# The high and low parts of the stationary operands of a gated FFN, laid element by element beside each other

## The chip, the core and the metric

The kernel runs on one core of a Trainium2 chip. The core has a matrix engine (PE, whose weight loads are shown apart as PEld), a vector engine (DVE), a scalar engine (ACT), a general engine (POOL) and a queue that issues transfers (SP). The metric is the device time of one launch in microseconds (us), the median of several runs. A matmul of PE takes two operands from on-chip memory: the stationary one (up to 128 × 128), which a weight load (LDWEIGHTS) puts into the array beforehand, and the moving one (up to 512 columns wide), which then streams past it. The result lands in PSUM.

## What is computed

First a chunked scan over sequences of 768 positions (4 batches, 8 heads, head size 32, state size 16), whose result is reshaped to 3072 tokens × 256. Then a gated FFN on these tokens, with 1536 hidden units:

```python
def reference(**kwargs):
    attn_out = _attn_ref(**attn_kwargs)              # (4, 8, 768, 32)
    x = attn_out.transpose(0, 2, 1, 3).reshape(B * S, H * D)   # (3072, 256)
    gate = 1.0 / (1.0 + np.exp(-(x @ w_gate)))       # w_gate (256, 1536)
    val = x @ w_val
    return (gate * val @ w_out).astype(np.float32)   # w_out (1536, 256)
```

The weights of the FFN arrive as 64-bit floats; the kernel turns them into 32-bit parts itself.

## The kernel before

The sequence is cut into 6 chunks of 128 positions, and a chunk of all 4 batches gives 512 tokens. The scan of a chunk (24 "units", one per chunk and batch) is made of small matmuls with work of DVE, ACT and POOL between them (lines 429 to 599), ahead of the chunk's FFN. PE does the FFN chunk by chunk, and the units of the next chunk are threaded in between. Chunk number is k, block of 128 hidden units is f (12 of them), and batch is j.

Precision decides the form of a matmul. From f = 6 of chunk 0 on, gate and value use pairs of parts: a value is held as a high part in the 32-bit format fp32r and a low part, what is left over, in the same format. Three products replace one: high × high, high × low, low × high. Some work of chunk 0 uses whole fp32 numbers instead.

- Gate and value, f < 6 of chunk 0 (lines 788 and 882): the stationary operand is a slice of the whole weights (tile `wr`), moving is `xw`, both fp32.
- Gate and value after that (line 891 in `products_of`): the stationary operand is a 128 × 128 slice of the parts `w` of a weight tile; moving are the parts `xh` and `xl` of the chunk's tokens, 512 columns. Six matmuls give one tile of 512 in PSUM, for the gate (`pg`) and then for the value (`pv`).
- From these, ACT makes the sigmoid `g` (832), DVE multiplies it with the value (853), ACT writes the high part of `h` (857) and POOL the low part (859). In chunk 0 DVE writes `h` whole, as fp32 (816, 849).
- Projection, chunk 0 (line 918 in `proj`): the stationary operand is a slice of the whole `h`, moving are whole weights, 256 columns.
- Projection of chunks 1 to 5: the stationary operand is the high part of `h`, moving are both parts of the weights side by side, 512 columns (929); then the low part of `h` under the high part of the weights, 256 columns (930). For the last 128 tokens the low part comes at the end (926, 937).

The parts of the weights are made by `part_w`: ACT writes the high part (390), POOL the low part (392), for 18 weight tiles, 12 of gate and value and 6 of the projection. A weight tile holds 2 × 256 numbers per partition and part. The whole weights from which they come lie in every second 32-bit word of their tile, since they are made in place from 64-bit numbers; so the matmuls of lines 788 and 882 read a stationary operand with a step of 8 bytes, and those of line 918 a moving one.

A planner (`run`) sets the order of all instructions when the program is built, from costs and due times; nothing of it is decided on the chip. Each engine then works through its list in order. Tiles of `h` and `w` lie in one pool (`hp`) under fixed tags, in buffers of 4 KiB per partition, which are reused from chunk to chunk.

The tiles that the change touches are made in these lines:

```python
w = hp.tile([P, 2, NK, 2 * P], F32R, ...)     # parts_of: part, k, column
hs[0, f] = hp.tile([P, 512], F32, ...)        # half_value and value: h of chunk 0, whole
hs[k, f] = hp.tile([P, 2, 512], F32R, ...)    # value: part, token
```

Of the kernel before, what the change touches and what calls it, by code (L numbers as in the profile page):

```python
# [8 lines left out]
F32 = mybir.dt.float32  # L9
F32R = mybir.dt.float32r  # L10
# [61 lines left out]
def tile_ssd_then_gated_ffn(  # L72
# [11 lines left out]
    nc = tc.nc  # L84
    NB, H, S, D = x.shape
    N = Bm.shape[-1]
    DM, DF = w_gate.shape
    wg32, wv32, wo32 = (w.bitcast(U32) for w in (w_gate, w_val, w_out))
    P = 128
# [5 lines left out]
    NK = DM // P  # L95
    NF = DF // P
# [9 lines left out]
    place = {i: n for n, i in enumerate(order)}  # L106
# [4 lines left out]
    hp = ctx.enter_context(tc.tile_pool(name="hp", bufs=1))  # L111
# [75 lines left out]
    def step(eng, cost, needs=(), makes=(), port=False, **buffers):  # L187

        return eng, cost, needs, makes, port, buffers
# [141 lines left out]
    raws, wgv, wo = {}, {}, {}  # L331
# [61 lines left out]

    def parts_of(i):
        if i < NF:
            w = hp.tile([P, 2, NK, 2 * P], F32R, tag=f"s{place[i]}", name=f"w{i}")
            wgv[i] = w
            return w[:, 0], w[:, 1]
        w = hp.tile([P, 2, 2, DM], F32R, tag=f"s{place[i]}", name=f"w{i}")
        wo[i - NF] = w  # L400
        return w[:, :, 0, :], w[:, :, 1, :]
# [359 lines left out]
    hs, xb, xw = {}, {}, []  # L761
# [12 lines left out]
    def thin(k, f):  # L774
        return k == 0 and f < NPLAIN

    def single(k, f):
        return k == 0 and f < NWHOLE

    def halved(k, f):  # L780
        return k == 0 and f < NHALF
# [24 lines left out]
    def half_value(f, i):  # L806
        yield step(
            "pe", GV0 / 2, [("whole", f // 2 * 2 + 1), ("pg", 0, f, i)], [("pv", 0, f, i)] + half_used(f, i, 1), port=8, banks=1
        )
        pm = half_of(f, i, 1)  # L810
        yield step("dve", DVE_HALF, [("sig", 0, f, i)], [("h", 0, f, i)], banks=-1, g=-1)
        g = gs.pop((0, f, i))
        if (0, f) not in hs:
            hs[0, f] = hp.tile([P, 512], F32, tag=f"h{f}", name=f"h0_{f}")
        by = "p (b l) -> p b l"
        nc.vector.tensor_tensor(
            out=hs[0, f].rearrange("p (b s l) -> p b s l", b=NB, s=2)[:, :, i], in0=pm[:, : 2 * P].rearrange(by, b=NB),
            in1=g[:, : 2 * P].rearrange(by, b=NB), op=ALU.mult,
        )

    def half_used(f, i, j):
        return [("used", f // 2 * 2 + j, i)] if f % 2 else []

    def all_used(q):
        return [("used", q, i) for i in range(2)] if q < NHALF else [("used", q)]
# [8 lines left out]
    def value(k, f):  # L834
        makes = [("pv", k, f)] + ([("gv", k)] if f == NF - 1 else [])
        yield step("pe", GV0 if thin(k, f) else GV_T / 2, needs_of(k, f, 1) + [("pg", k, f)], makes + used(k, f, 1), port=8 if thin(k, f) else 12, banks=1)
        pm = products_of(k, f, 1)
        held = []
        if k == 0:
            held = {  # L840
                4: [("S", b) for b in range(NB)], 5: [("cb", 1)], 6: [("cb", 3), ("cd", 2), ("cd", 3)],
                7: [("scan", 3)], 8: [("p",)], 9: [("a_p",)], 10: [("a_z",)],
            }.get(f, [])
            held += [n for i in range(NPLAIN) for n in all_used(i)] + [("xp", 1)] if f == NF - 1 else []
        if single(k, f):
            yield step("dve", DVE_MM, [("sig", k, f)] + held, [("h", k, f)], banks=-1, g=-1)
            g = gs.pop((k, f))
            hs[k, f] = hp.tile([P, 512], F32, tag=f"h{f}", name=f"h{k}_{f}")
            nc.vector.tensor_tensor(out=hs[k, f], in0=pm, in1=g, op=ALU.mult)
            return  # L850
        yield step("dve", DVE_MM, [("sig", k, f)], banks=-1)
        g = gs.pop((k, f))
        nc.vector.tensor_tensor(out=g, in0=pm, in1=g, op=ALU.mult)  # L853
        eng = yield step(("act", "dve"), (ACT_SB, DVE_1), [("proj", k - 1)] + held)
        hs[k, f] = hp.tile([P, 2, 512], F32R, tag=f"h{f}", name=f"h{k}_{f}")
        hh, hl = (hs[k, f][:, i] for i in range(2))
        copies[eng](hh, g)  # L857
        eng = yield step(("dve", "pool"), (DVE_SB, POOL_SB), [], [("h", k, f)], port=True, g=-1)
        engines[eng].tensor_tensor(out=hl, in0=g, in1=hh.bitcast(F32), op=ALU.subtract)  # L859

    def used(k, f, j):
        return [("used", f // 2 * 2 + j)] if thin(k, f) and f % 2 else []
# [12 lines left out]
    def products_of(k, f, j):  # L875

        fs = slice(f % 2 * P, (f % 2 + 1) * P)
        pm = ps_mm.tile([P, 512], F32, tag="mm", name=f"p{'gv'[j]}{k}_{f}")
        if thin(k, f):

            for kt in range(NK):
                nc.tensor.matmul(  # L882
                    pm, whole[f // 2 * 2 + j][:, kt, fs], xw[0][:, kt], start=(kt == 0), stop=(kt == NK - 1)
                )
            return pm
        xh, xl = xb[k]
        w = wgv[f // 2 * 2 + j]
        i = 0
        for kt in range(NK):
            for part, xx in ((0, xh), (0, xl), (1, xh)):  # L890
                nc.tensor.matmul(pm, w[:, part, kt, fs], xx[:, kt], start=(i == 0), stop=(i == 3 * NK - 1))  # L891
                i += 1
        return pm

# [2 lines left out]
    def proj(k, j):  # L897

        js = slice(j * P, (j + 1) * P)
        last = (k, j) == (NCH - 1, NB - 1)  # L900
        fs = [f for f in range(NF) if not single(k, f)] + [f for f in range(NF) if single(k, f)]
        for n, f in enumerate(fs):
            start, stop = n == 0, n == NF - 1
            if n % 4 == 0:
                some = fs[n : n + 4]
                needs = [n for i in some for n in ([("h", k, i, 0), ("h", k, i, 1)] if halved(k, i) else [("h", k, i)])]
                needs += sorted({("whole" if single(k, i) else "w", NF + i // 2) for i in some})
                if n == 0:
                    needs.append(("gv", k))
                yield step(  # L910
                    "pe", 0.92 if last else sum(0.45 if single(k, i) else PROJ_T / 12 for i in some), needs,
                    [("proj", k)] if j == NB - 1 and n + 4 == NF else [],
                    port=8 if last else 16, banks=int(n == 0),
                )
                if n == 0:
                    acc = ps_mm.tile([P, 512], F32, tag="mm", name=f"po{k}_{j}")
            if single(k, f):
                nc.tensor.matmul(  # L918
                    acc[:, :DM], hs[k, f][:, js], whole[NF + f // 2][:, f % 2], start=start, stop=stop,
                    skip_group_check=True,  # L920
                )
                continue
            hh, hl = (hs[k, f][:, i, js] for i in range(2))
            w = wo[f // 2][:, f % 2]
            if last:
                nc.tensor.matmul(acc, hh, w.rearrange("p i m -> p (i m)"), start=start, stop=stop)  # L926
                continue

            nc.tensor.matmul(acc, hh, w.rearrange("p i m -> p (i m)"), start=start, stop=False, skip_group_check=True)  # L929
            nc.tensor.matmul(acc[:, :DM], hl, w[:, 0, :], start=False, stop=stop, skip_group_check=True)  # L930
        o = wk.tile([P, DM], F32, tag="o", name=f"o{k}_{j}")
        if last:

            yield step("pe", 1.4, [], [("end",)], port=24, banks=1)
            low = ps_mm.tile([P, 512], F32, tag="mm", name="po")
            for f in range(NF):
                nc.tensor.matmul(
                    low[:, :DM], hs[k, f][:, 1, js], wo[f // 2][:, f % 2, 0, :], start=(f == 0), stop=(f == NF - 1)
                )
        if single(k, NF - 1):  # L940
            eng = yield step(("act", "dve"), (ACT_HALF, DVE_HALF), [], [], o=1, banks=-1)
            copies[eng](o, acc[:, :DM])
        else:
            yield step("act", ACT_HALF, [], [], o=1)
            nc.scalar.copy(o, acc[:, :DM])  # L945
            yield step("dve", DVE_HALF, banks=-1)
            nc.vector.tensor_tensor(out=o, in0=acc[:, DM:], in1=o, op=ALU.add)  # L947
        if last:
            yield step("dve", DVE_HALF)
            nc.vector.tensor_tensor(out=o, in0=low[:, :DM], in1=o, op=ALU.add)  # L950
        row = j * S + k * L
        yield step("sp", 0.52, port=0.4, o=-1)
        nc.sync.dma_start(out[row : row + P, :], o)
# [205 lines left out]
```

## Time and profile before

| | us |
|---|---|
| median of 3 runs | 370.71 |
| lowest, highest | 369.96, 372.96 |
| span of the profiled execution | 368.7 |

The profiled execution is one execution of the program under the hardware profiler, and no time of its own beside the span is known. The span reaches from its first to its last instruction, and is what the shares and the sums below refer to; the runs also hold what lies around it, so that the median is 2.0 us above the span.

The chunks lie in it as follows: gate and value of chunk 0 until 63 us, its projection until 89.8, then gate and value and projection of the chunks 1 to 5 by turns, the last projection from 348.4 on.

How to read the views: durations are those of single instructions; matmuls are pipelined, so that a matmul starts before the one ahead of it has drained, and durations of matmuls add up to more than the time that they take. The distance between two starts is the pace. "x" is a count. Behind the bar of a group stands the time for which the engine was idle just before such an instruction, and who ended it. A weight load has rows of its own under PEld and overlaps matmuls.

### The profile page before, as it was taken

To read this page: it belongs to the slowest core of one execution; us is meant where nothing else is said; L and a number is where in the kernel's file an instruction comes from. 1 tells how busy PE (TensorE), PEld (TensorE's weight loads), DVE (VectorE), ACT (ScalarE), POOL (GpSimd) and SP (SyncE) were. 2 spreads that over 40 slices of the span, in tenths; PEclk is the share of its full clock that TensorE was granted. 3 is DMA by queue.
4 is the path that set the end of the run, shared out by engine and by line. 5 is a ranking of instruction groups with operands and counts; after the bars stand their busy time and mean duration, and the time that the engine had idled before them with its cause. 6 is when DMAs were issued, how large, how long until landed. Compare 5 with 4: busy or idle time off the path is not lost.

```text
span 368.7 us, 8115 instructions
## 1 busy us (share of the span) xinstructions
PE 360.1 (98%) x3372; PEld 285.9 (78%) x3372; DVE 156.4 (42%) x278; ACT 150.2 (41%) x309; POOL 151.9 (41%) x160
## 2 busy tenths in 40 slices
PE   8989899999999999999999999999999999999996
PEld 3568378778887788778788887888877888888885
DVE  4778478675325751253452225422243510222201
ACT  2565985324565411544410454511445420343400
POOL 5436665746797410345420345530144240154410
PEclk9999999999999999999999999999999999999999
DMA  8999885627015331235031006321000000000000
GB/s 138 168 309 215 271 261 151 106 43 154 7 16 100 45 89 57 37 64 59 16 87 44 28 3 115 34 41 37 31 2 2 2 0 28 30 0 0 2 28 28
DMA packets 89270, 26.27 MB, mean 71 GB/s; under 512 B 76306, under 2 KB 82002, under 8 KB 89234
## 3 DMA queue, kind: packets, MB, share of 16 engines
q1 hardware_dynamic: 85074, 25.37, 30.9%
q10 hardware_dynamic: 4160, 0.39, 1.2%
q8 instruction: 26, 0.43, 0.5%
q14 instruction: 10, 0.08, 0.1%
HBM read 22.41 MB, written 3.34 MB: 70 GB/s over the span
## 4 chain that ended last, share of the span: by engine, by line
PE 87%; DMA 2%; SPq 2%; ACT 1%; DVE 1%; POOL 0%; issue 0%; POOLq 0%
PE pv L891 25%; PE pg L891 25%; PE po L929 15%; PE po L930 7%; PE po L918 6%; DMA wr<-in_moe_w_val_dram 2%; PE pcb L524 2%; PE pcb L579 2%; PE pcb L493 2%; SPq L299 1%; PE pcb L535 1%; PE pt L429 1%; PE po L926 1%; PE pv L882 1%; PE pt L430 1%; ACT wr L373 0%
## 5 line engine op out<-in xcount | busy, mean ns | idle before, releaser
L859 POOL TENSOR_TENSOR h<-g,h 128x512 fp32r<-128x512 f32 x60 | 78.8, 1314 | 153.4 <-ACT h L857 152.9
L891 PE MATMUL pv<-xh,w 128*128 128x512 f32 x264 | 94.0, 397 | 0.0
L891 PE MATMUL pg<-xh,w 128*128 128x512 f32 x264 | 93.7, 395 | 0.0
L853 DVE TENSOR_TENSOR g<-pv,g 128x512 f32<-128x512 f32 x60 | 41.5, 692 | 97.1 <-PE pv L891 94.1
L929 PE MATMUL po<-w,h 128*128 128x512 f32 x228 | 81.8, 402 | 0.0
L857 ACT CAST h<-g 128x512 fp32r<-128x512 f32 x60 | 37.2, 621 | 79.6 <-DVE g L853 79.6
L930 PE MATMUL po<-w,h 128*128 128x256 f32 x228 | 63.9, 280 | 0.0
L891 PEld LDWEIGHTS pg<-xh,w 128*128 128x128 f32 x264 | 49.5, 188 | 11.1 <-issue 0.4
L891 PEld LDWEIGHTS pv<-xh,w 128*128 128x128 f32 x264 | 49.6, 188 | 10.6 <-issue 0.5
L891 PE MATMUL pv<-xl,w 128*128 128x512 f32 x132 | 51.4, 390 | 0.0
L891 PE MATMUL pg<-xl,w 128*128 128x512 f32 x132 | 51.4, 390 | 0.0
L929 PEld LDWEIGHTS po<-w,h 128*128 128x128 f32 x228 | 42.8, 188 | 10.9 <-issue 0.3
L832 ACT ACTIVATE g<-pg 128x512 f32<-128x512 f32 x68 | 40.6, 598 | 13.9 <-PE pg L891 13.4
L930 PEld LDWEIGHTS po<-w,h 128*128 128x128 f32 x228 | 43.0, 189 | 0.2
L947 DVE TENSOR_TENSOR o<-po,o 128x256 f32<-128x256 f32 x20 | 8.5, 425 | 53.6 <-ACT o L945 53.6
L945 ACT COPY o<-po 128x256 f32<-128x256 f32 x20 | 7.4, 372 | 54.5 <-PE po L930 54.0
L392 POOL TENSOR_TENSOR w<-wr,w 128x512 fp32r<-128x512 f32 x18 | 25.6, 1427 | 8.5 <-ACT w L390 8.5
L891 PEld LDWEIGHTS pg<-xl,w 128*128 128x128 f32 x132 | 24.8, 188 | 5.1 <-issue 0.2
L891 PEld LDWEIGHTS pv<-xl,w 128*128 128x128 f32 x132 | 24.8, 188 | 4.5
L375 POOL TENSOR_TENSOR wr<-wr 128x512 int32<-128x512 int32 x18 | 20.2, 1129 | 14.3 <-ACT wr L373 8.6
L448 DVE TENSOR_TENSOR_SCAN ab<-ab,delta 128x512 f32<-128x512 f32 x20 | 24.1, 1216 | 1.9 <-DMA ab<-a_z 1.4
L918 PE MATMUL po<-wr,h 128*128 128x256 f32 x96 | 23.4, 393 | 0.0
(104 smaller groups left out, 367.9 us busy)
## 6 DMA issues: line engine op xcount, KB each, us to landing
ab<-a_z SPq DMA_DIRECT2D x40, 128.0 KB
wr<-in_moe_w_gate_dram SPq DMA_DIRECT2D x6, 512.0 KB
wr<-in_moe_w_val_dram SPq DMA_DIRECT2D x6, 512.0 KB
wr<-in_moe_w_out_dram SPq DMA_DIRECT2D x6, 512.0 KB
out_dram<-o SPq DMA_DIRECT2D x24, 128.0 KB
xn<-in_x_dram SPq DMA_DIRECT2D x10, 256.0 KB
bn<-in_B_dram SPq DMA_DIRECT2D x10, 128.0 KB
cn<-in_C_dram SPq DMA_DIRECT2D x10, 128.0 KB
```

Of the source, the lines that this page charges most:

```text
L375: nc.gpsimd.tensor_tensor(out=lw.bitcast(I32), in0=hw.bitcast(I32), in1=lw.bitcast(I32), op=ALU.add)
L392: engines[eng].tensor_tensor(out=lo, in0=lw, in1=hi.bitcast(F32), op=ALU.subtract)
L448: nc.vector.tensor_tensor_scan(out=t.rearrange("p h l -> p (h l)"), data0=t.rearrange("p h l -> p (h l)"), data1=delta.rearrange("p h l -> ...
L832: nc.scalar.activation(gs[k, f], pm, AF.Sigmoid)
L853: nc.vector.tensor_tensor(out=g, in0=pm, in1=g, op=ALU.mult)
L857: copies[eng](hh, g)
L859: engines[eng].tensor_tensor(out=hl, in0=g, in1=hh.bitcast(F32), op=ALU.subtract)
L891: nc.tensor.matmul(pm, w[:, part, kt, fs], xx[:, kt], start=(i == 0), stop=(i == 3 * NK - 1))
L918: nc.tensor.matmul(acc[:, :DM], hs[k, f][:, js], whole[NF + f // 2][:, f % 2], start=start, stop=stop, skip_group_check=True,)
L929: nc.tensor.matmul(acc, hh, w.rearrange("p i m -> p (i m)"), start=start, stop=False, skip_group_check=True)
L930: nc.tensor.matmul(acc[:, :DM], hl, w[:, 0, :], start=False, stop=stop, skip_group_check=True)
L947: nc.vector.tensor_tensor(out=o, in0=acc[:, DM:], in1=o, op=ALU.add)
```

## The change

The layout of the tiles of `w` (gate and value) and `h` changes. Where the high parts of a row stood together and the low parts behind them, a high part and its low part now lie in neighbouring 32-bit words. A slice of either part then has a step of 8 bytes. The tile of `h` in chunk 0, which has no parts, gets the same step: it takes every second word of a tile twice as large. The size of the buffers doesn't grow, since the tags had room for both parts. The parts of the projection's weights, which are moving operands, stay as they are, and so do the tokens `xh` and `xl`.

```diff
     def parts_of(i):
         if i < NF:
-            w = hp.tile([P, 2, NK, 2 * P], F32R, tag=f"s{place[i]}", name=f"w{i}")
+            w = hp.tile([P, NK, 2 * P, 2], F32R, tag=f"s{place[i]}", name=f"w{i}")
             wgv[i] = w
-            return w[:, 0], w[:, 1]
+            return w[:, :, :, 0], w[:, :, :, 1]
...
         if (0, f) not in hs:
-            hs[0, f] = hp.tile([P, 512], F32, tag=f"h{f}", name=f"h0_{f}")
+            hs[0, f] = hp.tile([P, 512, 2], F32, tag=f"h{f}", name=f"h0_{f}")[:, :, 0]
...
         if single(k, f):
...
-            hs[k, f] = hp.tile([P, 512], F32, tag=f"h{f}", name=f"h{k}_{f}")
+            hs[k, f] = hp.tile([P, 512, 2], F32, tag=f"h{f}", name=f"h{k}_{f}")[:, :, 0]
...
-        hs[k, f] = hp.tile([P, 2, 512], F32R, tag=f"h{f}", name=f"h{k}_{f}")
-        hh, hl = (hs[k, f][:, i] for i in range(2))
+        hs[k, f] = hp.tile([P, 512, 2], F32R, tag=f"h{f}", name=f"h{k}_{f}")
+        hh, hl = (hs[k, f][:, :, i] for i in range(2))
...
-                nc.tensor.matmul(pm, w[:, part, kt, fs], xx[:, kt], start=(i == 0), stop=(i == 3 * NK - 1))
+                nc.tensor.matmul(pm, w[:, kt, fs, part], xx[:, kt], start=(i == 0), stop=(i == 3 * NK - 1))
...
-            hh, hl = (hs[k, f][:, i, js] for i in range(2))
+            hh, hl = (hs[k, f][:, js, i] for i in range(2))
...
-                    low[:, :DM], hs[k, f][:, 1, js], wo[f // 2][:, f % 2, 0, :], start=(f == 0), stop=(f == NF - 1)
+                    low[:, :DM], hs[k, f][:, js, 1], wo[f // 2][:, f % 2, 0, :], start=(f == 0), stop=(f == NF - 1)
```

The planner's costs and due times stay, and the order of the instructions on every engine is the same as before. The line numbers are the same in both kernels.

## The prediction

> **What bounds the kernel now.** I read the page first (busy times, clock, chain), then busy time by stage, then durations by line, and last single instructions in the timeline.
>
> ```profile
> span 368.7 us, 8115 instructions
> PE 360.1 (98%) x3372; PEld 285.9 (78%) x3372; DVE 156.4 (42%) x278; ACT 150.2 (41%) x309; POOL 151.9 (41%) x160
> PEclk9999999999999999999999999999999999999999
> PE pv L891 25%; PE pg L891 25%; PE po L929 15%; PE po L930 7%; PE po L918 6%; DMA wr<-in_moe_w_val_dram 2%; PE pcb L524 2%; PE pcb L579 2%; PE pcb L493 2%; SPq L299 1%; PE pcb L535 1%; PE pt L429 1%; PE po L926 1%; PE pv L882 1%; PE pt L430 1%; ACT wr L373 0%
> ```
>
> The matrix engine is busy 98% of the span at the full clock, and the chain that ended last runs through the matmuls of the gated FFN: L891 (gate and value), L929, L930 and L926 (projection of chunks 1 to 5), L918 (projection of chunk 0). By stage (columns: stretch, length, then busy us and count of PE, PEld, DVE, ACT, POOL; then clock, DMA share, GB/s):
>
> ```profile
> 100.00:110.00 10.00, 10.00 (x46) 8.25 (x45) 2.46 (x4) 7.02 (x14) 9.35 (x8) 1.00 0.09 9
> 127.00:204.00 77.00, 77.00 (x813) 63.50 (x798) 29.58 (x57) 23.50 (x51) 21.03 (x23) 1.00 0.29 58
> 204.00:355.00 151.00, 151.00 (x1283) 123.88 (x1282) 44.55 (x81) 56.16 (x112) 52.18 (x48) 1.00 0.10 21
> ```
>
> Where these stretches lie, PE has no idle time. So the time changes by what the change does to the pace of PE, unless another engine falls far enough behind to stop it.
>
> The change touches only the operand that PE holds still. Of those, the first stage (L788, L882) reads 8-byte-stepped weights already, so its rows price the new form. Columns here: engine, operation, count, then shortest/median/longest in ns.
>
> ```profile
> L788 PEld LDWEIGHTS pv<-xw,wr x32: 194/196/197, 17.7 to 35.7; 128*128 128x128 f32 x32
> L788 PE MATMUL pg<-xw,wr x32: 379/379/492, 15.9 to 33.9; 128*128 128x256 f32 x32
> L882 PE MATMUL pv<-xw,wr x8: 592/592/705, 37.8 to 45.1; 128*128 128x512 f32 x8
> L209 PE MATMUL fill<-eye x4: 592/594/697, 15.0 to 17.7; 128*128 128x512 f32 x4
> L918 PEld LDWEIGHTS po<-wr,h x96: 186/188/192, 62.7 to 89.6; 128*128 128x128 f32 x96
> L918 PE MATMUL po<-wr,h x96: 385/387/493, 63.0 to 89.8; 128*128 128x256 f32 x96
> L891 PEld LDWEIGHTS pv<-xl,w x132: 187/188/192, 47.1 to 347.7; 128*128 128x128 f32 x132
> L891 PE MATMUL pv<-xl,w x132: 387/389/398, 47.3 to 347.9; 128*128 128x512 f32 x132
> L929 PE MATMUL po<-w,h x228: 389/398/504, 127.1 to 362.6; 128*128 128x512 f32 x114
> L930 PE MATMUL po<-w,h x228: 274/281/284, 127.4 to 362.8; 128*128 128x256 f32 x114
> L926 PE MATMUL po<-w,h x12: 389/395/398, 358.2 to 363.6; 128*128 128x512 f32 x12
> ```
>
> L788 and L918 are both fp32, 256 columns wide. L788 (stepped stationary, moving data in contiguous runs) takes 379 ns, L918 (contiguous stationary, moving weights stepped) 387. A quick reader concludes that a stepped stationary operand saves 8 ns a matmul. Two things say otherwise. L209 holds a contiguous stationary operand under contiguous moving data, and takes 594 against 592 of L882, whose weights are stepped: the same. And the excess is there when no weights are being loaded at all. Three matmuls, each the last before a unit's small matmuls, whose loads wait:
>
> ```profile
> 18.74 0.38 PE L788 MATMUL pv<-xw,wr 128*128 128x256 f32 x1
> 19.05 0.13 PEld L493 LDWEIGHTS pcb<-bct 32*64 32x64 f32 x2 [0.33 <-ACT bct L657]
> ...
> 52.36 0.39 PE L891 MATMUL pg<-xh,w 128*128 128x512 f32 x1
> 52.68 0.13 PEld L493 LDWEIGHTS pcb<-bct 32*64 32x64 f32 x2 [0.35 <-issue]
> ...
> 66.36 0.39 PE L918 MATMUL po<-wr,h 128*128 128x256 f32 x1
> 66.68 0.11 PEld L524 LDWEIGHTS pcb<-m,xn 64*32 64x32 f32 x2 [0.35 <-DVE wr L369]
> ```
>
> Between each matmul's start and the next load nothing is loaded, yet L891 and L918 still take 0.39 us and hold up what follows by 0.32, against 0.38 and 0.31 of L788. What L891 and L918 share, and L788, L882 and L209 do not, is how fast the moving stream runs through memory. A column costs (592 − 379) / 256 = 0.83 ns in fp32 (L882, L788) and (398 − 281) / 256 = 0.46 in fp32r (L929, L930): fp32r reads its words twice as fast, and L918 reads fp32 words that lie twice as far apart. So I read the 8 to 10 ns as a cost of the moving operand, which the change leaves as it is.
>
> **The change part by part.** No instruction is added, removed or moved on any queue: PE, DVE, ACT, POOL and SP hold the same instructions in the same order. Only addresses inside tiles change.
>
> (1) Weight loads. 792 loads at L891, 228 each at L929 and L930, 12 each at L926 and L937, 96 at L918 get the step: 1,368. Each lasts 196 ns in place of 188 by L788 against L918, 8 more. That counts only where a load isn't covered by the matmul before it. Under 512 columns it is covered: L788's matmuls last 379 both next to a 196 ns load and, above, without one, and they follow each other at the pace that their columns set. Two places remain.
>
> (1a) Loads after a unit's small matmuls stand bare. The longest matmul of a line includes such a bare load: L918 493 − 387 = 106 ns and L929 504 − 398 = 106 for contiguous weights, L788 492 − 379 = 113 and L882 705 − 592 = 113 for stepped ones: 7 ns more each. The waits of the units' loads count the places:
>
> ```profile
> PEld pcb L493 <- issue: 3.5, 10, 0.4
> PEld pcb L579 <- issue: 3.2, 10, 0.4
> PEld pcb L524 <- issue: 2.9, 9, 0.4
> ```
>
> 29 × 7 ns = 0.2 us.
>
> (1b) L930's matmul is only 256 columns wide, and the load of the next L929 has to go beside it:
>
> ```profile
> 200.11 0.19 PEld L929 LDWEIGHTS po<-w,h 128*128 128x128 f32 x1
> 200.23 0.19 PEld L930 LDWEIGHTS po<-w,h 128*128 128x128 f32 x1
> 200.46 0.19 PEld L929 LDWEIGHTS po<-w,h 128*128 128x128 f32 x1
> 200.57 0.19 PEld L930 LDWEIGHTS po<-w,h 128*128 128x128 f32 x1
> ```
>
> The load beside L930 has 0.12 and 0.11 us until the next one starts. A bare load needs 106 now and 113 then. If the load sets that pace already, all 228 (and 12 of L937) lose 7 ns: 240 × 7 = 1.7 us. If the matmul sets it, 113 still fits: 0. The two gaps of 120 and 110 ns stand around 113, so only the shorter ones should lose a few ns: I take a quarter of the bound, 0.4 us.
>
> By the Trainium skill (SBUF — State Buffer, Door 1: The DMA port swizzle) reads keep full bandwidth as long as two of them fall into each 16-byte line; an 8-byte step of fp32 gives just two. By that rule (1) would be 0, and the sum 0 in place of 0.6. The trace differs from it by the 196 against 188.
>
> (2) Matmuls. Same columns, same moving operands. 0 from the argument above; the bounds are rivals A and B.
>
> (3) Writers. ACT's cast, POOL's subtraction and DVE's product of chunk 0 now write (POOL also reads) every second word.
>
> ```profile
> L859 POOL TENSOR_TENSOR h<-g,h 128x512 fp32r<-128x512 f32 x60 | 78.8, 1314 | 153.4 <-ACT h L857 152.9
> L392 POOL TENSOR_TENSOR w<-wr,w 128x512 fp32r<-128x512 f32 x18 | 25.6, 1427 | 8.5 <-ACT w L390 8.5
> L857 ACT CAST h<-g 128x512 fp32r<-128x512 f32 x60 | 37.2, 621 | 79.6 <-DVE g L853 79.6
> L390 ACT CAST w<-wr 128x512 fp32r<-128x512 f32 x18 | 11.9, 661 | 0.0
> ```
>
> L392 and L390 have one stepped operand already, and L859 and L857 none: +113 ns on POOL and +40 on ACT bound the price. So a tile of h comes at most 0.15 us later. What covers it: POOL waits 152.9 us in all for ACT's h. The cover is thinnest in chunk 1, from 100 to 110 us, where POOL is busy 9.35 of 10 because the weights' parts and h are made by turns. There 12 tiles of h at 113 ns add up to 1.4 us of lateness. Chunk 1's last h and the matmuls that go before its use:
>
> ```profile
> 128.08 1.29 POOL L859 TENSOR_TENSOR h<-g,h 128x512 fp32r<-128x512 f32 x1 [1.44 <-ACT h L857]
> ...
> 131.31 0.50 PE L929 MATMUL po<-w,h 128*128 128x512 f32 x1
> ```
>
> POOL stood idle 1.44 us before this last h, so the lateness has been made up by then; and the matmuls from 131.31 on still read h of f 4 to 7, so f 11, done at 129.37, has over 2 us to spare. With that cover gone 1.4 us would come on top; below, nothing can be gained from writers off the path. I take 0.
>
> Sum: 0.2 + 0.4 + 0 = +0.6 us, so a span of 369.3. The profiled span of 368.7 stands 2.0 below the median of the runs (370.71); with the same 2.0 around it the forecast is **371.3 us**.
>
> **Rivals.**
>
> A, faster: the stationary step, not the moving stream, makes the excess, and the change removes it. For it: L788 and L882 are the only full-width loads with the step, and the only full-width matmuls of the FFN without the excess. Against it: L209, and the excess without a load. Price: 792 × (389 − 379) = 7.9; L929 228 × (398 − 379) = 4.3; L930 at half the columns and so half of L929's excess or a little less, 228 × 9 = 2.1; L918 96 × 8 = 0.8; L926 12 × 16 = 0.2. Together 15.3 us, and 355.4 us. The Trainium skill (TensorE: Matmul & The Clock Gate, Back-to-back issue gap) gives about 216 ns from one warm 512-column matmul to the next and names no type; by it the excess of L891 is nothing that fp32r must pay, and the sum would be A's 355.4 us in place of 371.3. No run here shows an fp32r matmul at that pace.
>
> B, slower: a stepped load spreads over twice the bytes, and collides with a moving stream that has no slack. In the first stage the moving stream goes at half the pace, so its rows can't exclude it. Against it: with a contiguous load beside it L891 lasts 389, without one 0.39 (no cost seen). Price, from L926 against L891 (the same width under other operands, 395 − 389): 792 + 228 + 12 matmuls × 6 = 6.2 us, with (1b) in full 1.7 and (1a) 0.2: 8.1 us, 378.8. It decides from 3.7 us, 1%, on: that is 2.7 ns for each of the 1,368 loads. The far end, L929's longest under load against L891's (about 14 ns), gives 11 us and 382; I think it unlikely.
>
> C, POOL gets late enough in chunk 1 that PE waits: 1.4 us from (3), 372.7. It ends inside the same 1%.
>
> **How the numbers follow.** The forecast (with C) gets 0.70, A 0.13, B 0.17. A measurement of this kernel can tell about 1% (3.7 us) from no change. Of B's share I put 0.01 under that: same 0.71, faster 0.13, slower 0.16. The forecast's own bounds are 370.7 (every term 0) to 370.7 + 0.2 + 1.7 + 1.4 = 374.0. The range starts at 369.0, since the runs before scatter from 369.96 upwards, and goes to 379.0, so that it takes in B's price: 0.70 and most of 0.17. It leaves out A and B's far end.
>
> **What would show it.** Right: the loads of L891, L929, L930 and L918 at 194 to 197 ns; matmuls of L891 still 387 to 389 and of L918 387; starts of L930's neighbours no more than 7 ns further apart; POOL's h between 1,314 and 1,430 and no wait of PE for it. If L891 falls to about 379, A is right and my reading of the moving stream is wrong. If L891 rises to 395 or more with the loads unchanged in number, B is. If the matmuls keep their durations but the loads beside L930 grow, (1b) was too small.

## The result, and the profile after

| | before | after |
|---|---|---|
| median of 4 runs, us | 370.63 | 375.47 |
| lowest, highest, us | 369.96, 372.96 | 374.08, 376.83 |
| ratio of the times, 95% interval | | 1.0132, 1.0087 to 1.0177 |
| span of the profiled execution, us | 368.7 | 372.3 |

The kernel became slower by 1.3%. The time lies inside the predicted range (369.0 to 379.0), 4.2 us above the forecast, and on the side of rival B. The medians mix executions at two clocks: with a mean granted clock of 0.998 or more the kernel before took 370.3 us in the median and below that 372.3 (26 executions), after 374.1 and 376.8; one execution of 710.8 us, of the later kernel with stepped low parts, is left out of its ratio.

The head of the page of after: PE is still busy 98% of the span, at the full clock throughout, with the same number of instructions.

```profile
span 372.3 us, 8115 instructions
PE 363.5 (98%) x3372; PEld 293.3 (79%) x3372; DVE 158.6 (43%) x278; ACT 153.1 (41%) x309; POOL 156.6 (42%) x160
PEclk9999999999999999999999999999999999999999
```

The durations by line of after, to be laid beside those of the prediction (count, then shortest/median/longest in ns, then first and last start in us):

```profile
L788 PE MATMUL pg<-xw,wr x32: 379/379/492, 14.8 to 33.0; 128*128 128x256 f32 x32
L918 PEld LDWEIGHTS po<-wr,h x96: 193/194/196, 62.2 to 89.1; 128*128 128x128 f32 x96
L918 PE MATMUL po<-wr,h x96: 386/387/504, 62.4 to 89.3; 128*128 128x256 f32 x96
L891 PEld LDWEIGHTS pv<-xl,w x132: 193/193/199, 46.2 to 351.2; 128*128 128x128 f32 x132
L891 PE MATMUL pv<-xl,w x132: 392/394/396, 46.5 to 351.4; 128*128 128x512 f32 x132
L929 PE MATMUL po<-w,h x228: 392/395/512, 127.5 to 366.1; 128*128 128x512 f32 x114
L930 PE MATMUL po<-w,h x228: 276/281/283, 127.8 to 366.3; 128*128 128x256 f32 x114
L926 PE MATMUL po<-w,h x12: 392/394/399, 361.8 to 367.1; 128*128 128x512 f32 x12
```

The loads of all stepped operands became 5 to 8 ns longer; 8 had been forecast. But only one line's matmuls became longer: L891, from 389 to 394 ns. L918 (387), L930 (281) and L926 (395 to 394) stand, and L929 lost 3. Durations thus show only a few ns on one line, so the next thing to read is the pace. In chunk 5 there are no units between the matmuls. The first gate matmul of that chunk and the first projection matmul behind its last value, in the timeline of before:

```profile
315.71 0.40 PE L891 MATMUL pg<-xh,w 128*128 128x512 f32 x1
...
348.36 0.39 PE L929 MATMUL po<-w,h 128*128 128x512 f32 x1
```

and of after:

```profile
317.94 0.40 PE L891 MATMUL pg<-xh,w 128*128 128x512 f32 x1
...
351.86 0.40 PE L929 MATMUL po<-w,h 128*128 128x512 f32 x1
```

144 matmuls lie between: 32.65 us before, 226.7 ns each; 33.92 us after, 235.6 ns each. That is 1.27 us in this chunk alone, 8.9 ns for each matmul, more than in the other chunks. Over the whole trace, between neighbouring matmuls of L891 that start less than 300 ns apart (734 in both kernels), the mean distance went from 227.8 to 233.6 ns: 734 × 5.8 = 4.3 us. The 27 longer distances, which hold a bare load, went from 339.3 to 347.0: 0.2 us. The 19 matmuls of L891 ahead of a unit's small matmuls went from about 319 to 326: 0.1 us (two of them took 327 before already, two took 320 after). L929 and L930 together went from 352.1 to 351.1 ns a pair: −0.2 us. The sum is 4.4 us. From the first matmul of L788 (15.9 before, 14.8 after) to the end of the span there are 352.8 us before and 357.5 after: 4.7 us. The spans differ by only 3.6, since the first stage began 1.1 us earlier in the profiled execution of after.

The writers, from the groups of after:

```profile
L859 POOL TENSOR_TENSOR h<-g,h 128x512 fp32r<-128x512 f32 x60 | 79.8, 1331 | 156.3 <-ACT h L857 156.2
L857 ACT CAST h<-g 128x512 fp32r<-128x512 f32 x60 | 39.5, 659 | 81.5 <-DVE g L853 81.5
L392 POOL TENSOR_TENSOR w<-wr,w 128x512 fp32r<-128x512 f32 x18 | 28.5, 1589 | 7.5 <-ACT w L390 7.4
```

POOL's h costs 17 ns more, ACT's 38, POOL's parts of the weights 162. POOL still waits 156.2 us for ACT's h, and no wait of PE for either of them came up. So the loss is in PE's own pace, at L891.

### The profile page after: what moved, and what is told of

Its sections match the earlier page's. It is cut to its first block, busy times and chain, and to the rows that moved or that the text cites. A ratio compares the mean times of both kernels' runs of the same rounds, so it can differ in the third digit from the quotient of the medians.

```text
span 372.3 us, 8115 instructions
## 1 busy us (share of the span) xinstructions
PE 363.5 (98%) x3372; PEld 293.3 (79%) x3372; DVE 158.6 (43%) x278; ACT 153.1 (41%) x309; POOL 156.6 (42%) x160
## 4 chain that ended last, share of the span: by engine, by line
PE 94%; DMA 3%; ACT 1%; DVE 1%; issue 0%
PE pv L891 25%; PE pg L891 25%; PE po L929 15%; PE po L930 7%; PE po L918 6%; DMA xn<-in_x_dram 2%; PE pcb L524 2%; PE pcb L493 2%; PE pg L788 2%; PE pv L788 2%; PE pcb L579 2%; PE pcb L535 1%; DMA cn<-in_C_dram 1%; PE pv L882 1%; PE pg L882 1%; PE pt L429 1%
## 5 line engine op out<-in xcount | busy, mean ns | idle before, releaser
L859 POOL TENSOR_TENSOR h<-g,h 128x512 fp32r<-128x512 f32 x60 | 79.8, 1331 | 156.3 <-ACT h L857 156.2
L891 PE MATMUL pv<-xh,w 128*128 128x512 f32 x264 | 95.4, 402 | 0.0
L891 PE MATMUL pg<-xh,w 128*128 128x512 f32 x264 | 95.0, 400 | 0.0
L929 PE MATMUL po<-w,h 128*128 128x512 f32 x228 | 81.6, 400 | 0.0
L857 ACT CAST h<-g 128x512 fp32r<-128x512 f32 x60 | 39.5, 659 | 81.5 <-DVE g L853 81.5
L930 PE MATMUL po<-w,h 128*128 128x256 f32 x228 | 64.0, 281 | 0.0
L891 PEld LDWEIGHTS pg<-xh,w 128*128 128x128 f32 x264 | 51.2, 194 | 11.0 <-issue 0.4
L891 PEld LDWEIGHTS pv<-xh,w 128*128 128x128 f32 x264 | 51.3, 194 | 10.4 <-issue 0.3
L891 PE MATMUL pg<-xl,w 128*128 128x512 f32 x132 | 52.0, 394 | 0.0
L891 PE MATMUL pv<-xl,w 128*128 128x512 f32 x132 | 52.0, 394 | 0.0
L929 PEld LDWEIGHTS po<-w,h 128*128 128x128 f32 x228 | 44.5, 195 | 8.8 <-issue 0.3
L930 PEld LDWEIGHTS po<-w,h 128*128 128x128 f32 x228 | 44.8, 197 | 0.2
L392 POOL TENSOR_TENSOR w<-wr,w 128x512 fp32r<-128x512 f32 x18 | 28.5, 1589 | 7.5 <-ACT w L390 7.4
L891 PEld LDWEIGHTS pg<-xl,w 128*128 128x128 f32 x132 | 25.6, 194 | 4.9 <-issue 0.2
L891 PEld LDWEIGHTS pv<-xl,w 128*128 128x128 f32 x132 | 25.7, 194 | 4.5
L918 PE MATMUL po<-wr,h 128*128 128x256 f32 x96 | 23.5, 394 | 0.0
```

The lines of the kernel that those rows point to most:

```text
L392: engines[eng].tensor_tensor(out=lo, in0=lw, in1=hi.bitcast(F32), op=ALU.subtract)
L891: nc.tensor.matmul(pm, w[:, kt, fs, part], xx[:, kt], start=(i == 0), stop=(i == 3 * NK - 1))
L918: nc.tensor.matmul(acc[:, :DM], hs[k, f][:, js], whole[NF + f // 2][:, f % 2], start=start, stop=stop, skip_group_check=True,)
```

## The experiments

Each kernel ran beside the kernel before on the same chip. "Pace" is the mean distance between starts of neighbouring L891 matmuls, worked out as above (only distances under 300 ns; for the moving x, whose matmuls start further apart, those under 520).

| kernel | time, us | before, us | ratio, 95% interval | pace, ns |
|---|---|---|---|---|
| before | | 370.63 | | 227.8 |
| after | 375.47 | 370.63 | 1.0132, 1.0087 to 1.0177 | 233.6 |
| step in w alone | 375.25 | 370.51 | 1.0118, 1.0083 to 1.0153 | 233.5 |
| step in h alone | 371.15 | 370.51 | 1.0006, 0.9981 to 1.0031 | 228.1 |
| w in other rows, no step | 370.49 | 370.51 | 0.9995, 0.9971 to 1.0020 | 227.8 |
| step in the gate's w alone | 374.14 | 370.51 | 1.0084, 1.0056 to 1.0112 | 231.1 |
| step in the low parts of w | 373.26 | 371.32 | 1.0061, 1.0036 to 1.0086 | 231.1 |
| step in the high parts of w | 375.20 | 371.06 | 1.0117, 1.0082 to 1.0153 | 233.0 |
| step of 16 bytes in w | 382.19 | 371.32 | 1.0271, 1.0228 to 1.0314 | 235.2 |
| step in the moving x | 547.43 | 371.32 | 1.4736, 1.4691 to 1.4781 | 453 |
| other moving array at L918 | 370.65 | 371.32 | 0.9967, 0.9941 to 0.9993 | 227.8 |
| output weights in a row at L918 | 369.55 | 371.06 | 0.9960, 0.9940 to 0.9980 | 227.7 |

### Which of the two tiles: w alone, h alone

The first question was which half of the change costs the time. The kernel before, with the new layout for the tile of w only:

```diff
-            w = hp.tile([P, 2, NK, 2 * P], F32R, tag=f"s{place[i]}", name=f"w{i}")
+            w = hp.tile([P, NK, 2 * P, 2], F32R, tag=f"s{place[i]}", name=f"w{i}")
...
-            return w[:, 0], w[:, 1]
+            return w[:, :, :, 0], w[:, :, :, 1]
...
-                nc.tensor.matmul(pm, w[:, part, kt, fs], xx[:, kt], start=(i == 0), stop=(i == 3 * NK - 1))
+                nc.tensor.matmul(pm, w[:, kt, fs, part], xx[:, kt], start=(i == 0), stop=(i == 3 * NK - 1))
```

> Only the parts of the gate and value weights get the step of 8 bytes; h stays contiguous. Theory S (a stepped weight load beside a full-pace fp32r stream makes each matmul of L891 about 6.7 ns longer, and nothing else costs): L891 pace 233 ns and duration 394, L929, L930 and L918 as before, about 375.4 us in all, the whole loss. Rival H (the stepped h makes the loss, through the loads beside the 256-column matmuls of L930 or through later h): about 370.7 us, L891 at 389. Rival T (half and half): about 373.

And the rest of the change without it: the edits of h, with the three lines above as before.

> Only h gets the step of 8 bytes (all chunks); the weights' parts stay as before. Theory S: L891 stays at 389, loads of L929 and L930 go to 195 ns, the pair of L929 and L930 goes from 353 to about 350 ns as in the changed kernel (228 x 3 ns = 0.7 us less), so 370.0 to 370.7 us. Rival H: about 375 us. Rival T: about 373.

The first took 1.0118 times as long, the second 1.0006. So the whole loss comes from w, read at L891, and the step of h costs nothing that can be measured, though its loads are longer there too. By line, with the step in w alone:

```profile
L891 PE MATMUL pv<-xl,w x132: 392/394/399, 47.5 to 353.3; 128*128 128x512 f32 x132
```

and with the step in h alone:

```profile
L918 PEld LDWEIGHTS po<-wr,h x96: 193/194/197, 62.6 to 89.6; 128*128 128x128 f32 x96
L918 PE MATMUL po<-wr,h x96: 386/388/504, 62.9 to 89.8; 128*128 128x256 f32 x96
L930 PEld LDWEIGHTS po<-w,h x228: 193/196/201, 127.2 to 362.6; 128*128 128x128 f32 x114
L930 PE MATMUL po<-w,h x228: 276/281/283, 127.5 to 362.8; 128*128 128x256 f32 x114
```

At L918, L929 and L930 a load of 194 or 196 ns in place of 188 thus doesn't by itself lengthen the matmul beside it. This kernel also has the slower writers of h (POOL 1,328 and ACT 656 ns in the mean), so they are cleared as well. The slower writers of w's parts are cleared by their time: they end before 115 us in both kernels, before and after, and from 204 to 315 us L891's pace is still 233 ns after against 228 before.

### Step or place: the same parts in other rows

A new layout also moves every operand to another address. Here the parts change places by rows of 1 KiB, and each slice stays contiguous.

```diff
-            w = hp.tile([P, 2, NK, 2 * P], F32R, tag=f"s{place[i]}", name=f"w{i}")
+            w = hp.tile([P, NK, 2, 2 * P], F32R, tag=f"s{place[i]}", name=f"w{i}")
...
-            return w[:, 0], w[:, 1]
+            return w[:, :, 0], w[:, :, 1]
...
-                nc.tensor.matmul(pm, w[:, part, kt, fs], xx[:, kt], start=(i == 0), stop=(i == 3 * NK - 1))
+                nc.tensor.matmul(pm, w[:, kt, part, fs], xx[:, kt], start=(i == 0), stop=(i == 3 * NK - 1))
```

> The parts of the gate and value weights lie at other addresses (part inside k, 1 KiB apart in place of 2 KiB), but each slice is contiguous as before. Theory S: loads 188 ns, L891 389 ns, 370.7 us (no change). Rival D (where a slice lies against the moving operand makes the cost, not its step): L891 moves off 389, to 392 or more, and the time by 2 us or more.

0.9995, pace 227.8. So it is the step that costs, and not that the parts lie elsewhere.

### A price for each load, or for the stream: gate alone, low parts alone, high parts alone

If each stepped load had a fixed price, half of them would cost half. First the step for the gate's weights alone (the even tiles):

```diff
-            w = hp.tile([P, 2, NK, 2 * P], F32R, tag=f"s{place[i]}", name=f"w{i}")
-            wgv[i] = w
+            w = hp.tile([P, 2, NK, 2 * P] if i % 2 else [P, NK, 2 * P, 2], F32R, tag=f"s{place[i]}", name=f"w{i}")
+            wgv[i] = w = w if i % 2 else w.rearrange("p k f i -> p i k f")
```

> Only the parts of the gate's weights get the step; those of the value stay contiguous. Theory S with a cost in each matmul beside a stepped load: of six matmuls in a row those whose next load is stepped take 233 ns, the others 227, and the time is half the loss, about 373.1 us. Rival P (the step shifts the phase at which all matmuls of L891 start, and the cost is one of the phase): gate and value get the same pace, either both 233 (375.4 us) or both 227 (370.7 us).

It took 1.0084 times as long, 3.1 us, with bounds of 2.1 and 4.2, which hold half of the loss of 4.8. In its rows gate and value stand apart:

```profile
L891 PEld LDWEIGHTS pg<-xl,w x132: 192/193/299, 46.4 to 349.9; 128*128 128x128 f32 x132
L891 PE MATMUL pg<-xl,w x132: 392/394/399, 46.7 to 350.2; 128*128 128x512 f32 x132
L891 PEld LDWEIGHTS pv<-xl,w x132: 187/188/192, 48.1 to 351.3; 128*128 128x128 f32 x132
L891 PE MATMUL pv<-xl,w x132: 387/389/402, 48.3 to 351.5; 128*128 128x512 f32 x132
L891 PE MATMUL pv<-xh,w x264: 388/392/504, 48.0 to 351.8; 128*128 128x512 f32 x132
```

The matmuls of a gate tile run as in after (394); those of a value tile run as before (389) or, in the rows under `xh`, partly so (392). The mean distance is 233.0 ns inside a gate tile and 228.9 inside a value tile, and in between where one follows the other (232 from gate to value, 231 from value to gate). The 19 places ahead of a unit's small matmuls divide cleanly: 326 or 327 ns at all 10 behind a gate tile, 318 or 319 at all 9 behind a value tile. So the rival of one pace for both fell, and the slow pace comes and goes within a few matmuls. Inside a tile of six that left open whether it belongs to the matmul whose own operand is stepped, or to the one beside which the stepped load runs. L891 uses the parts in the order high, high, low, so a step in the low parts alone mixes them one by one:

```diff
-            w = hp.tile([P, 2, NK, 2 * P], F32R, tag=f"s{place[i]}", name=f"w{i}")
-            wgv[i] = w
-            return w[:, 0], w[:, 1]
+            w = hp.tile([P, 2, NK * 2 * P], F32R, tag=f"s{place[i]}", name=f"w{i}")
+            wgv[i] = w[:, 0].rearrange("p (k f) -> p k f", k=NK), w[:, 1].rearrange("p (f k) -> p k f", k=NK)
+            return wgv[i]
...
-                nc.tensor.matmul(pm, w[:, part, kt, fs], xx[:, kt], start=(i == 0), stop=(i == 3 * NK - 1))
+                nc.tensor.matmul(pm, w[part][:, kt, fs], xx[:, kt], start=(i == 0), stop=(i == 3 * NK - 1))
```

> The kernel before, with only the low parts of the gate and value weights stepped by 8 bytes (the low parts of two channel tiles lie beside each other; the high parts stay contiguous). L891 multiplies in the order high, high, low, so one matmul in three has a stepped stationary operand. Both theories of a price per load: 264 of the 792 matmuls, 264 x 6.6 ns = 1.7 us, about 372.2. Theory Own (the matmul that uses a stepped operand takes longer): from the start of a low-part matmul to the next start 233 ns, the other two 227, and the matmul ahead of L493, which is a low-part one, still takes 327. Rival Next (the load beside it takes the time from the matmul that streams): 233 for the second high-part matmul, under which the stepped load runs, and 227 for the low-part one, 318 ahead of L493. If neither shows and all starts are near 227, the price needs all operands to be stepped, and the time is 370.5.

Neither shape showed. The median distances were 231 ns from the first high part, 230 from the second and 233 from the low part, close together (227, 227 and 227 before), and a third of the stepped loads brought a pace of 231.1, over half of the whole rise. The ratio stands for 2.3 us, where 1.7 were expected; its interval, 1.3 to 3.2, holds both. The matmul ahead of a unit's small matmuls, a stepped one, took 326 to 328 at all 19 places, which spoke for a price on one's own operand. The mirror of it, with the step in the high parts, puts a contiguous one there:

```diff
-            wgv[i] = w[:, 0].rearrange("p (k f) -> p k f", k=NK), w[:, 1].rearrange("p (f k) -> p k f", k=NK)
+            wgv[i] = w[:, 0].rearrange("p (f k) -> p k f", k=NK), w[:, 1].rearrange("p (k f) -> p k f", k=NK)
```

> The mirror of the run with stepped low parts: only the high parts of the gate and value weights have a step of 8 bytes, two of three stationary operands of L891; the low parts are contiguous. Theory Own (the price belongs to the matmul whose own operand is stepped): the matmul ahead of L493, a low-part one, takes 318 ns to the next start, as before, although all the loads ahead of it but one are stepped; in after and with stepped low parts it takes 326 to 327. Rival Phase (the price is a state of the whole stream): 326 to 327 there too. In both the time lies between that with stepped low parts (L891's starts 13 ns longer for three matmuls) and after (20 ns for three): 264 x 13 to 20 ns = 3.4 to 5.3 us as bounds, 373.3 to 375.5.

The timeline of this kernel at such a place (the last matmul before L493 multiplies by a contiguous low part, and nothing is loaded beside it):

```profile
52.32 0.40 PE L891 MATMUL pg<-xl,w 128*128 128x512 f32 x1
52.55 0.40 PE L891 MATMUL pg<-xh,w 128*128 128x512 f32 x1
52.88 0.23 PEld L493 LDWEIGHTS pcb<-bct 32*64 32x64 f32 x16 [0.37 <-issue]
```

0.40 us, and 0.33 to the next: all 19 places of this kind took 326 to 328 ns. So the price isn't tied to the matmul that owns the stepped operand, and a load beside it isn't needed either. I read it as a state that the stream of matmuls gets into and that lasts for some matmuls: with the gate alone it is gone at the end of the next tile of six. What that state is, no run shows. Nor need a step be the only way into it: two of the 19 places took 327 in the kernel before, where L891's operands have none. Two thirds of the loads with a step bring nearly all of it (233.0 of 233.6), one third over half.

### The size of the step: 16 bytes

```diff
-            w = hp.tile([P, 2, NK, 2 * P], F32R, tag=f"s{place[i]}", name=f"w{i}")
+            w = hp.tile([P, 2 * P, NK, 2], F32R, tag=f"s{place[i]}", name=f"w{i}")
...
-            return w[:, 0], w[:, 1]
+            return tuple(w[:, :, :, part].rearrange("p c k -> p k c") for part in range(2))
...
-                nc.tensor.matmul(pm, w[:, part, kt, fs], xx[:, kt], start=(i == 0), stop=(i == 3 * NK - 1))
+                nc.tensor.matmul(pm, w[:, fs, kt, part], xx[:, kt], start=(i == 0), stop=(i == 3 * NK - 1))
```

> The kernel before, with a step of 16 bytes in the stationary operands of L891 instead of 4 (after has 8). Theory Dose (the price follows the bytes that a load reaches over: 512 B costs nothing extra, 1 KiB costs 6.6 ns): 2 KiB cost 3 x 6.6 = 20 ns for each of 792 matmuls, 15.7 us, about 386, L891 at about 408 ns, its loads at 205 or more. Rival Gate (a step is either 4 bytes or not): as after, L891 394 ns, loads 193, about 375.3. Wider writes by ACT and POOL could add to either, and show as waits of PE.

By line, with the step of 16 bytes:

```profile
L891 PEld LDWEIGHTS pv<-xh,w x264: 307/310/330, 50.0 to 360.7; 128*128 128x128 f32 x132
L891 PE MATMUL pv<-xh,w x264: 387/400/632, 50.0 to 360.9; 128*128 128x512 f32 x132
L891 PEld LDWEIGHTS pv<-xl,w x132: 308/310/338, 50.2 to 360.5; 128*128 128x128 f32 x132
L891 PE MATMUL pv<-xl,w x132: 394/398/403, 50.4 to 360.7; 128*128 128x512 f32 x132
```

Both theories missed. A load takes 310 ns in place of 188, where one theory had 193 and the other put its price on the matmul; but the matmuls stand at 398 to 400, far from 408, and the pace rose only to 235.2: a load that lasts longer than the distance between two matmuls still hides almost wholly under them. Where it stands bare it shows: the longest matmul is 632 − 400 = 232 ns over the median, against 500 − 389 = 111 before. L891's distances add up to 10.2 us more than before, 727 × 7.3 ns = 5.3 from the pace and 4.9 from distances over 300 ns, bare loads above all (27 × 0.12 = 3.3). The rest are two long distances early on (1.21 us in place of 0.63, and 0.58 where PE waits for POOL's low part) and five of about 350 ns later. The writes of the parts had become longer: ACT's took 1,110 ns (median) in place of 661 (mean), POOL's 1,864 (median) in place of 1,427 (mean). The ratio stands for 10.1 us (8.5 to 11.7).

### The moving operand: x with a step, L918 without one

The prediction put the excess of 8 to 10 ns in the old kernel on the moving operand. Two runs try that side. In the first the moving operand of L891 gets the step, by the same layout for the parts of x:

```diff
-                xb[c] = [wk.tile([P, NK, 512], F32R, tag=f"x{p}", name=f"x{p}{c}") for p in "hl"]
+                xi = wk.tile([P, NK, 512, 2], F32R, tag="xi", name=f"xi{c}")
+                xb[c] = [xi[:, :, :, i] for i in range(2)]
```

(and the same for chunk 0)

> The kernel before, with the high and low parts of x, L891's moving operand, beside each other element by element (a step of 8 bytes), and the stationary operand contiguous as before. Theory Dose (a matmul pays for the bytes that its operands reach over, moving and stationary alike): the moving operand reaches over 4 KiB instead of 2, at least 13 ns more for each of 792 matmuls, 381 or more, L891 at 402 ns or more. Rival Load (only the stationary side pays): L891 389 ns, pace 227, 370.5.

By line; the new lines shift L891 to L893:

```profile
L893 PEld LDWEIGHTS pv<-xi,w x396: 186/208/209, 49.4 to 525.6; 128*128 128x128 f32 x198
L893 PE MATMUL pv<-xi,w x396: 629/632/702, 49.5 to 526.1; 128*128 128x512 f32 x198
```

The matmuls took 632 ns in place of 389, at a pace of 453, twice the old one. The direction was as expected and the size was not: at least 13 ns were expected, and 225 came. So this stream of fp32r, 512 columns wide, runs at half speed when its moving operand has a step of 8 bytes.

In the second, L918 gets a contiguous moving operand:

```diff
-                    acc[:, :DM], hs[k, f][:, js], whole[NF + f // 2][:, f % 2], start=start, stop=stop,
+                    acc[:, :DM], hs[k, f][:, js], xb[0][0].bitcast(F32)[:, f % 2, : DM], start=start, stop=stop,
```

> The kernel before, with another, contiguous array in place of L918's moving operand, which has a step of 8 bytes (chunk 0's projection then multiplies by parts of x instead of its weights). It tries the prediction's sentence that the excess of L918 over L788 (387 against 379 ns) is a cost of the moving operand. Theory Moving: L918 takes 379 ns at a pace of 216 instead of 227, 89 x 11 ns = 1.0 us less, about 369.5. Rival Other (the excess belongs to something else at that place): 387, 227, 370.5.

```profile
L918 PEld LDWEIGHTS po<-xh,h x96: 186/190/192, 64.1 to 90.0; 128*128 128x128 f32 x96
L918 PE MATMUL po<-xh,h x96: 377/379/483, 64.3 to 90.2; 128*128 128x256 f32 x96
```

387 became 379, and the median distance of two starts 216 in place of 227. So L918's excess was a cost of its moving operand. The time fell by 0.33% (interval 0.07 to 0.59%), in line with the 1.0 us expected.

### A version that beats both

That excess can be had without leaving anything out. In chunk 0 the tiles of h fill half of their buffers, and the whole output weights fit into the other half; POOL then writes its sum there, contiguous, in place of every second word of the raw tile. h of f = 5 to 10 was chosen because their buffers are taken again only after the parts have been made from these weights.

```diff
+        to = lw.bitcast(F32)
+        if i >= NF:
+            to = h_first(i - NF + 5)[:, 1].rearrange("p (f m) -> p f m", f=2)
-        nc.gpsimd.tensor_tensor(out=lw.bitcast(I32), in0=hw.bitcast(I32), in1=lw.bitcast(I32), op=ALU.add)
+        nc.gpsimd.tensor_tensor(out=to.bitcast(I32), in0=hw.bitcast(I32), in1=lw.bitcast(I32), op=ALU.add)
...
+    def h_first(f):
+        if f not in firsts:
+            firsts[f] = hp.tile([P, 2, 512], F32, tag=f"h{f}", name=f"h0_{f}")
+        return firsts[f]
...
-            hs[0, f] = hp.tile([P, 512], F32, tag=f"h{f}", name=f"h0_{f}")
+            hs[0, f] = h_first(f)[:, 0]
...
```

> A kernel meant to beat both: the kernel before, with the output weights that chunk 0 multiplies by written by POOL into free contiguous space beside chunk 0's h, so that L918's moving operand has no step. Nothing is left out. From the run with another array in that place: L918 at 379 ns and a pace of 216 instead of 227, 89 x 11 ns = 1.0 us less, about 369.6. Rival: the new space ties POOL's add to the reads of h, or delays chunk 1's h, and PE waits there: 370.6 or more.

By line; L918 is L926 here, and its names differ only because the weights lie in h's buffers:

```profile
L926 PE MATMUL po<-h,h x80: 377/379/483, 62.8 to 88.6; 128*128 128x256 f32 x80
L926 PE MATMUL po<-h x16: 379/379/379, 76.6 to 88.2; 128*128 128x256 f32 x16
```

L918's median distance is 216, and the time 369.55 against 371.06: 0.4% less, with an interval of 0.2 to 0.6%, which is 0.7 to 2.2 us where 1.0 was expected. This is the fastest kernel of the study, if by little.

## Why the prediction was right or wrong

**What bounds the kernel.** Right: PE is busy 98% in both kernels, and the time moved by what PE's pace moved.

**(1) Weight loads.** Right in kind and nearly in size: 193 to 196 ns against 194 to 197 forecast. (1a), the bare loads: 0.2 us forecast, 27 distances × 7.7 ns = 0.2 measured. (1b), the loads beside L930's short matmuls: 0.4 forecast, 0 measured. The mean distance from L930 to the next L929 stayed at 117 ns, although the loads that go beside L930 (those of L929) grew from 188 to 195; the lower bound held.

The Trainium skill (SBUF — State Buffer, Door 1: The DMA port swizzle) asks for at least two accesses to each 16-byte line for full bandwidth, which an 8-byte step of fp32 gives and a 16-byte step doesn't. For loads that fits the sizes here but for some ns (188, 193 and 310 ns at steps of 4, 8 and 16 bytes), and so it does for ACT's writes of w at 8 and 16 (672 ns in the mean, and 1,110 in the median). For the matmul it doesn't fit: L891 paid 5.8 ns at 8 bytes on the stationary side, and 225 on the moving side. The measurement decides.

**(2) Matmuls: the step that failed.** "Same columns, same moving operands. 0 from the argument above." It measured 734 × 5.8 ns and the distances ahead of small matmuls, 4.4 us, nearly the whole loss. By the prediction's own sign L891 had to stay at 387 to 389 ns, and it came out at 394. One observation of the argument held: the old excess of L918 is the moving operand's, as the two runs without its step show. That L891's old excess is of the same kind wasn't tried. What didn't follow is that a cost of the moving operand leaves no room for one of the stationary operand: a step there slowed L891 by 5.8 ns. The rows that the prediction had for a stepped stationary operand, L788 and L882, are fp32, and fp32 didn't show the cost after the change either: L918, with the step in h, stayed at 387 ns and at a median distance of 227.

What bore on it was set aside rightly and then not weighed: the prediction said that the first stage can't exclude rival B, since its fp32 stream goes at half the pace. The row used against B, L891 without a load at 0.39, holds for contiguous loads only. After the change the same place reads 0.40, again with nothing loaded beside it:

```profile
51.59 0.40 PE L891 MATMUL pg<-xh,w 128*128 128x512 f32 x1
51.92 0.21 PEld L493 LDWEIGHTS pcb<-bct 32*64 32x64 f32 x12 [0.36 <-issue]
```

So the absence of a cost without a load beside it, in a kernel with contiguous loads, couldn't say what stepped ones would do.

**(3) Writers.** Right: +17 ns on L859 (bound 113), +38 on L857 (bound 40), no wait of PE. L392's +162 went past the 113, but PE didn't wait for it.

**Rival A** fell: L891 didn't go to 379, and the one line that got shorter, L929, did so by 3 ns. The Trainium skill (TensorE: Matmul & The Clock Gate, Back-to-back issue gap) gives about 216 ns as the gap of a warm 512-column matmul taken by itself, and about 131 as measured in a sustained stream, and names no type for either. Here fp32 at L918 reaches 216 for its 256 columns once its moving operand is contiguous, and L891, fp32r with 512 columns, had no mean pace under 227.7 in any run.

**Rival B** had the right sign and, for L891, the right size: 792 × 6 = 4.8 us priced, 4.4 measured. That the size fits is luck: the 6 ns were the difference between two lines that both had contiguous operands, and L926, from which it came, didn't get longer with the step (395 to 394). Rival B was wrong in two ways besides. L929, L926 and (1b), 3.1 of its 8.1 us, paid nothing. And a collision between a load and the matmul beside it is not what the runs show: with the step in the high parts alone, a matmul with a contiguous operand and no load beside it pays too. Its sign for itself, L891 at 395 or more, came out as 394.

**Rival C** didn't happen: with the step in h alone the time is that of before.

**The chances.** "Within 1%" had 0.71; the ratio is 1.0132, with 1.0087 as its lower end. The forecast's own bounds, 370.7 to 374.0, missed the 375.5. The range held only because it reached to B's price; for the forecast's own mechanism that is luck.

**What stays open.** Why L891's stream slows when its stationary operands have a step isn't settled, and that it is a state of the stream is a reading, not shown. The distances move in small steps: where the pace is steady, three neighbouring matmuls of L891 take 680 ns before, 693 or 694 with the low parts stepped, and 700, 706 or 707 after, so these levels lie about 6.7 ns apart or a multiple of it. Why L929, an fp32r matmul of the same width with a 256-column one between, pays nothing wasn't tried. The matmul between can't be the whole reason: L926, fp32r, 512 columns and nothing between, starts 232.2 ns apart before and 232.9 after (nine distances). Both lines hold h and stream weights, and L926 was at about 232 before any step.

## What to carry to other kernels

Interleaving two parts element by element need not be free for a matrix engine's operands, even where the loads look covered: at L891, an fp32r stream of 512 columns, an 8-byte step in the stationary operand cost 2.5% of the pace, and in the moving operand it doubled the time, while in h, the stationary operand of L929 and L926, it cost nothing. Leave matmul operands contiguous where no run has shown the step to be free, and where buffers are half empty use them to make a stepped moving operand contiguous. A row in which the partner runs at half the pace, as L788's here, didn't show what the new access pattern would cost: price it in the stream that will see it, and give the rival whose evidence is missing more than a small chance.

## What the runs showed of the hardware that was not expected

- A weight load of L891 grows little from a step of 4 to 8 bytes (188 to 193 ns) and much at 16 (310 ns), and even then hides almost wholly under matmuls that start every 235 ns.
- An fp32r moving operand of 512 columns with an 8-byte step halves the speed of the matmul (632 against 389 ns; pace 453 against 228), while with an fp32 one of 256 columns it loses 5% (216 to 227).
- The price of stepped stationary operands at L891 doesn't add up by loads: a third of them brings 3.3 ns of pace, half 3.2, two thirds 5.1, all 5.8.
